# A spectral and expert-retrieval layer in one kernel: two blocks of tokens looked up row by row, with u and v rows in one fetch and part of the checks moved

## The chip, the cores and the metric

The kernel runs on one core of a Trainium2 chip. Its time is the device time of one execution in microseconds (us): before the change the median of 3 runs is 1177.19 us (1176.13 to 1178.46). The profiled execution is one more run, with a time of its own.

## The reference, cut to what matters

2048 tokens x of 512 numbers are normalised; the output is x plus a Fourier mixing of them (part A) plus an expert layer (part B):

```python
xn  = layernorm(x)
A   = dft_seq_re @ (xn @ dft_hid_re.T) - dft_seq_im @ (xn @ dft_hid_im.T)
q   = einsum("nd,dhc->nhc", xn, w_q)             # 32 heads, two halves of 128
s1, s2 = q1 . k1, q2 . k2                        # 64 keys each
# the 2 best of the 2 x 2 best sums s1 + s2 name 2 of 4096 experts per head
g   = softmax(top_s)
act = gelu(einsum("nd,nhkd->nhk", xn, u[top_e]))
out = x + A + einsum("nhk,nhk,nhkd->nd", g, act, v[top_e])
```

So every token uses 64 rows of u and the same 64 rows of v, each of 512 floats.

## The kernel before, in words

The tokens are 16 blocks of 128. The work has three parts.

The opening transforms the tokens and prepares the first weights. The **score part** runs over 8 chunks of 4 heads (j) and, in each, over 16 blocks (i): twelve matmuls per step (L705), a copy to SBUF on ScalarE (L710), and on VectorE the best values and their indices (L713, L717). Between the steps ScalarE and GpSimd (POOL) split weights into two 16-bit parts (`m_prep`, L158 to L166; `fill_uv`, L608 to L610), and POOL and VectorE turn the indices into experts and gates (`routing`, L641 to L685).

The **block part** (from L1143) does most blocks densely. For block b, `u_part` (L834) multiplies all 4096 rows of u with the tokens in eight groups of 48 matmuls; ScalarE applies gelu (L837) into `act`. `g_mm` spreads the gates over the experts: VectorE builds L and R by comparisons (L860, L865, L868) from `cmp`, PE multiplies them (L870). `w_part` forms gate times activation (L878 on VectorE, L882 on ScalarE, L883 on VectorE), and `v_part` (L890) multiplies with v, 96 matmuls into one PSUM bank `v`. `finish` (L909) has VectorE read that bank, add the residual and store. `compact` transposes the indices of a later block on PE into a bank `zt` (L694), from which ScalarE makes `cmp` (L695). The loop at L1156 does, for each b: v of b beside w and g of b + 1; finish of b; zt of b + 2; u and half of g of b + 2. I call what lies between one zt and the next a cycle. `v` and `zt` are taken from the same two PSUM banks, tag "pc".

NB = 15 blocks are dense. The last one (NS = 1) is **picked**: 64 rows of u and 64 of v per token are fetched by indirect DMAs of 128 rows of 2 KB, issued by POOL (L914) into 5 buffers. First 64 dots on VectorE (L943), then one gelu over all 64 slots and a product with the gates, then 64 gains: ScalarE scales a row of v (L954), POOL adds it (L955). `pick` (L967) spreads these steps over the turns of the cycles, 16 a cycle; `follow` ties their order on VectorE and ScalarE behind a matmul, without a wait.

Beside it run **checks**: 68 comparing steps (`compare`, L980, and `compare_w`, L1032) load parts of the Fourier matrices (L987, L988), test their symmetry on VectorE (L989 to L1029) and sum the deviations on ScalarE (L1030); 60 `fit` steps (L1070) look at the size of weights on ScalarE. They use the 4 buffers of tag "w", as `w_part` does. Five comparing steps fall to a cycle, on odd turns and on one even turn of v.

A scheduler in the framework orders each engine's instructions from the program's order and the dependencies; engines then run in that order and wait on semaphores. DMAs issued by SP, and those issued by POOL, each stand in their engine's order.

Of the kernel before, what the change touches and what calls it, by code (L numbers as in the profile page):

```python
# [32 lines left out]
NS = 1  # L33
# [3 lines left out]
def tile_fnet_peer(ctx, tc, x, ca, cb, c5, wt, wf, wr, wq, kt, ut, un, vn, out):  # L37
# [52 lines left out]
    NF = NW + 32 + NCH - 1  # L90
    sums_sb = cst.tile([P, 138 + NF + 3], F32, name="sums")
# [459 lines left out]
    def part_b(safe, stS, stP, stE, xt, u_sb, cmp_p):  # L551
# [146 lines left out]

        def scores(j, i, vals, idx):
# [3 lines left out]
            for kd in range(KD):  # L703
                for l, r in ((0, 0), (0, 1), (1, 0)):
                    nc.tensor.matmul(ps, xt[i][:, l, kd, :], m[:, r, kd, :], start=(n == 0),  # L705
                                     stop=(n == 3 * KD - 1))
                    n += 1
# [12 lines left out]
            return st[:, 512:]  # L720
# [29 lines left out]
        for (which, g), n in zip(fills, slots):  # L750
            todo[n].append(lambda at, w=which, g=g: fill_uv(w, g, at))
            todo[n - (3 if n < 113 else 1)].append(lambda at, w=which, g=g: fill_load(w, g))
        m_stage(1, wq_tile, 0)
        pend = None
        for j in range(NCH):
# [5 lines left out]
            for i in range(NT):  # L761
                spare = scores(j, i, vals, idx)
# [48 lines left out]
        AHEAD = 5  # L811
# [84 lines left out]
        def follow(i, after):  # L896
            tc.add_manual_dep(i, after.ins.name, mybir.DependencyInfo(
                mybir.DependencyClass.NoSync, mybir.DependencyReason.DATA), reason="pace")

# [12 lines left out]
        def gather(table, n, s):  # L912
            t = bp.tile([P, D], F32, tag="ga", name=f"ga{n}_{s}", bufs=5)
            nc.gpsimd.indirect_dma_start(  # L914
                out=t, out_offset=None, in_=table,
                in_offset=bass.IndirectOffsetOnAxis(ap=eix[:, n].rearrange("p k h -> p (k h)")[:, s:s + 1], axis=0))
            return t

        def picked(n):

            b = NB + n
            N = 2 * H
            G = {}
            T = {}

            def fetch(s):
                if s < 2 * N:
                    G[s] = gather((un, vr)[s // N], n, s % N)

            def begin():  # L930
                xs = T["x"] = bp.tile([P, D], F32, tag="xs", name=f"xs_{n}", bufs=1)
                o = T["o"] = bp.tile([P, D], F32, tag="ov", name=f"ov{n}", bufs=1)
                T["z"] = bp.tile([P, N], F32, tag="za", name=f"za{n}", bufs=1)
                nc.sync.dma_start(xs, x[b // 4, b % 4])
                nc.sync.dma_start(o, y_d[b])
                nc.gpsimd.dma_start(o, x[b // 4, b % 4], accum_op=ALU.add)
                for s in range(AHEAD):
                    fetch(s)
                norm(xs, xs, b)

            def dot(s):
                t = G.pop(s)
                nc.vector.scalar_tensor_tensor(t, t, 1.0, T["x"], op0=ALU.mult, op1=ALU.mult,  # L943
                                               accum_out=T["z"][:, s:s + 1])
                fetch(s + AHEAD)

            def gate():
                za = T["z"]
                nc.scalar.activation(za, za, AF.Gelu_apprx_tanh)
                nc.gpsimd.tensor_tensor(za, za, gts[:, n].rearrange("p k h -> p (k h)"), op=ALU.mult)  # L950

            def gain(s):
                t = G.pop(N + s)
                nc.scalar.activation(t, t, AF.Copy, scale=T["z"][:, s:s + 1])  # L954
                nc.gpsimd.tensor_tensor(T["o"], T["o"], t, op=ALU.add)  # L955
                fetch(N + s + AHEAD)

            return [begin, *(lambda s=s: dot(s) for s in range(N)), gate, *(lambda s=s: gain(s) for s in range(N)),
                    lambda: nc.sync.dma_start(out[b * P:(b + 1) * P], T["o"])]

        vr = vn.rearrange("c p d -> (c p) d")
        picks = [] if safe else [f for n in range(NS) for f in picked(n)]
        more = [range(1, 1 + max(0, n - k * (NB - 2) - 4)) for n, k in ((68, 5), (NF - NCH + 1, 4))]
# [13 lines left out]

        later = []

        def compare(n):  # L980

            ri, g, kk = n // 32, n // 8 % 4, n % 8
            odd = kk // 4
            t = bp.tile([P, 4, 4, 64], F32, tag="w", name=f"cx{n}", bufs=WB)
            tf = t.rearrange("p s q c -> p (s q c)")
            tv = t.rearrange("p s q c -> p s (q c)")
            nc.sync.dma_start(tf[:, :P], ca[ri, g, :, kk * P:(kk + 1) * P])  # L987
            nc.sync.dma_start(tf[:, P:], cb[ri, g, kk].rearrange("p b c -> p (b c)"))  # L988
            nc.vector.tensor_reduce(asum[:, n:n + 1], tf[:, :P], axis=AX.X, op=ALU.add,  # L989
                                    apply_absolute_value=True)  # L990
            sgn = (((1, 1, 1), (-1, 1, -1)), ((-1, -1, 1), (1, -1, -1)))[ri][odd]
            ops = [ALU.subtract if v > 0 else ALU.add for v in sgn]
            op = ops[1]
            if g == 0:
                nc.vector.tensor_tensor(tv[:, 1], tv[:, 1], tv[:, 0], op=ops[0])
                for i in (2, 3):
                    nc.vector.scalar_tensor_tensor(tv[:, i], tv[:, 0], not0, tv[:, i], op0=ALU.mult, op1=ops[i - 1])  # L997
                f = (-1 if ri else 1) * sgn[1] * sgn[2]
                nc.vector.tensor_tensor(tv[0:1, 3], tv[0:1, 3], tv[0:1, 2],
                                        op=ALU.subtract if f > 0 else ALU.add)  # L1000
            else:
                sets = {}
                for i, o in enumerate(ops):
                    sets.setdefault(o, []).append(i + 1)
                for o, ix in sets.items():
                    sl = slice(ix[0], ix[-1] + 1, ix[1] - ix[0] if len(ix) > 1 else 1)
                    v = tv[:, sl]
                    nc.vector.tensor_tensor(v, v, tv[:, 0:1].to_broadcast([P, len(ix), 256]), op=o)  # L1008
            m = ALU.add if ri else ALU.subtract

            def mirror(v):

                c = 0 if kk else 1
                nc.vector.tensor_tensor(v[:, 2:4, c:], v[:, 2:4, c:], v[:, 0:2, c:], op=m)  # L1014
                if c:
                    nc.vector.tensor_tensor(v[:, 3, 0:1], v[:, 3, 0:1], v[:, 2, 0:1], op=m)

            if g == 0:
                mirror(t[0:1, 2])
                if odd and ri:  # L1020

                    nc.vector.tensor_copy(t[0:1, 2, 0:2], t[0:1, 0, 0:2])
# [5 lines left out]
            if kk == 0:  # L1028
                nc.vector.memset(t[:, 0, 2, 0:1], 0.0)  # L1029
# [308 lines left out]
```

## Time and profile before

| | us |
|---|---|
| median of 3 runs | 1177.19 |
| profiled execution, its time | 1171.21 |
| span of its instructions | 1169.3 |
| the cycles, from the end of block 0 to the end of block 13 | 526.7 to 1141.8 |
| PE busy, of the span | 1118.0 |
| VectorE busy | 987.5 |
| ScalarE busy | 632.3 |
| POOL busy | 488.1 |

A row of a group of instructions reads: line, engine, operation, what is written and read, shapes, count | busy us, mean ns of one | idle time of the engine just before them, and what ended it. A busy share is an average over parts with different limits, so the prediction reads the score part and the cycles apart.

### The profile page before, as it was taken

What the parts mean: (1) busy time and instruction counts of PE and PEld (TensorE: products, weight loads), DVE (VectorE), ACT (ScalarE), POOL (GpSimd) and SP (SyncE); (2) the same over time, 40 slices, a digit from 0 to 9 for tenths busy, and PEclk for the clock granted to TensorE, in tenths of its full rate; (3) what the DMA queues carried; (4) which work ended last, traced back from release to release, by engine and by line L of the source; (5) the groups of instructions that cost most, each with busy time, mean ns of one, the idle gap of its engine ahead of it and who ended that gap; (6) DMA issues with size and microseconds to landing.
All of it is one profiled execution on the core that took longest, in us unless ns stands there. A gap on an engine that the chain in (4) does not pass through costs nothing.

```text
span 1169.3 us, 29061 instructions
## 1 busy us (share of the span) xinstructions
PE 1118.0 (96%) x11681; PEld 734.0 (63%) x11681; DVE 987.5 (84%) x2946; ACT 632.3 (54%) x995; POOL 488.1 (42%) x411
## 2 busy tenths in 40 slices
PE   5799999999999999979999999999998999989997
PEld 4354555454454448939668578687685876858763
DVE  7878888798898997887998887988899689879895
ACT  2575546767767663443543534534546465464563
POOL 0021525548548342131343222323374666656742
PEclk9899999999999999989999999999999999999999
DMA  8254224132231113223554745645536456364554
GB/s 311 78 211 151 85 79 162 55 108 89 93 110 55 55 62 127 58 80 102 169 179 146 217 143 151 202 138 174 181 104 175 132 162 173 109 192 137 158 148 109
DMA packets 74369, 157.02 MB, mean 134 GB/s; under 512 B 10086, under 2 KB 26989, under 8 KB 74224
## 3 DMA queue, kind: packets, MB, share of 16 engines
q1 hardware_dynamic: 61522, 117.30, 30.1%
q0 software_dynamic: 12544, 37.76, 12.4%
q8 instruction: 93, 1.52, 0.5%
q14 instruction: 52, 0.43, 0.1%
q10 hardware_dynamic: 158, 0.01, 0.0%
HBM read 141.08 MB, written 13.96 MB: 133 GB/s over the span
## 4 chain that ended last, share of the span: by engine, by line
PE 71%; DVE 17%; DMA 4%; ACT 4%; issue 3%; SPq 0%; POOL 0%; DVEq 0%; ACTq 0%; POOLq 0%
PE s L705 27%; PE z L834 22%; PE v L890 14%; DVE L L860 3%; PE g L870 3%; DVE act L883 2%; DMA cx<-in_cb_dram 2%; DVE w L878 2%; ACT act L882 2%; DVE R L865 2%; PE m L144 2%; PE p L366 2%; DVE R L868 1%; DVE cx L1008 1%; DVE cx L997 1%
## 5 line engine op out<-in xcount | busy, mean ns | idle before, releaser
L834 PE MATMUL z<-xb,u 128*128 128x128 f16 x5760 | 335.1, 221 | 15.0 <-ACT act L837 12.6
L705 PE MATMUL s<-m,xq 128*128 128x512 f16 x1536 | 338.9, 379 | 0.0
L834 PEld LDWEIGHTS <-u 128*128 128x128 f16 x5760 | 327.6, 99 | 16.1 <-issue 13.3
L890 PE MATMUL v<-v,act 128*128 128x512 f16 x1440 | 319.7, 380 | 0.0
L705 PEld LDWEIGHTS <-xq 128*128 128x128 f16 x1536 | 148.4, 98 | 171.3 <-issue 0.2
L890 PEld LDWEIGHTS <-act 128*128 128x128 f16 x1440 | 138.2, 98 | 160.5 <-issue 1.9
L860 DVE TENSOR_TENSOR L<-io_lam,cmp 128x2048 f16<-128x2048 f16 x120 | 152.6, 1271 | 62.5 <-PE g L870 52.8
L837 ACT ACTIVATE act<-z,scl 128x512 f32<-128x512 f32 x120 | 81.9, 685 | 197.0 <-PE z L834 196.8
L914 POOL DMA_INDIRECT ga<-in_un_dram,eix x64 | 81.7, 1276 | 219.3 <-DVE ga L943 182.0
L713 DVE MAX8 vals<-ss 128x8 f32<-128x64 f32 x1024 | 152.6, 216 | 19.4 <-ACT ss L710 19.2
L955 POOL TENSOR_TENSOR ov<-ov,ga 128x512 f32<-128x512 f32 x64 | 98.3, 1535 | 114.0 <-ACT ga L954 112.4
L710 ACT ACTIVATE ss<-s,wsc 128x512 f32<-128x512 f32 x112 | 75.5, 680 | 81.8 <-PE s L705 71.7
L882 ACT ACTIVATE act<-w 128x1024 f16<-128x1024 f32 x60 | 79.5, 1351 | 54.5 <-DVE w L878 52.0
L717 DVE FIND_INDEX8 idx<-vals,ss 128x8 uint16<-128x256 f32 x256 | 107.1, 418 | 0.0
L914 POOL DMA_INDIRECT ga<-in_vn_dram,eix x64 | 89.2, 1393 | 34.7 <-DVE ga L943 17.3
L1030 ACT ACTIVATE cx<-cx 128x896 f32<-128x896 f32 x64 | 60.5, 946 | 67.4 <-DVE cx L1014 40.6
L883 DVE TENSOR_TENSOR act<-w,act 128x1024 f16<-128x1024 f32 x60 | 81.8, 1363 | 14.3 <-ACT act L882 14.1
L865 DVE TENSOR_TENSOR R<-io_c,cmp 128x512 f16<-128x512 f16 x120 | 81.5, 679 | 0.0
L878 DVE SCALAR_TENSOR_TENSOR w<-act,scl,g 128x1024 f32<-128x1024 f32 x60 | 75.4, 1276 | 2.2 <-PE g L870 1.8
L870 PEld LDWEIGHTS <-L 128*128 128x128 f16 x1920 | 56.4, 96 | 20.2 <-issue 8.0
L870 PE MATMUL g<-R,L 128*128 128x32 f16 x1920 | 58.6, 176 | 10.2 <-DVE R L868 7.8
L166 POOL TENSOR_TENSOR wq<-wq,wh 128x1024 f16<-128x1024 f32 x26 | 55.5, 2133 | 19.1 <-DMA wq<-in_wq_dram 16.4
(271 smaller groups left out, 1241.0 us busy)
## 6 DMA issues: line engine op xcount, KB each, us to landing
cx<-in_cb_dram SPq DMA_DIRECT2D x64, 448.0 KB, 4.4
wq<-in_wq_dram SPq DMA_DIRECT2D x32, 512.0 KB, 6.5
fit<-in_wq_dram SPq DMA_DIRECT2D x28, 512.0 KB, 5.4
uv<-in_ut_dram SPq DMA_DIRECT2D x16, 512.0 KB, 3.7
uv<-in_vn_dram SPq DMA_DIRECT2D x16, 512.0 KB, 3.7
xq<-in_x_dram SPq DMA_DIRECT2D x8, 512.0 KB
xt_d<-xq SPq DMA_DIRECT2D x16, 256.0 KB, 4.1
cx<-in_ca_dram SPq DMA_DIRECT2D x64, 64.0 KB, 2.5
```

Of the source, the lines that this page charges most:

```text
L705: nc.tensor.matmul(ps, xt[i][:, l, kd, :], m[:, r, kd, :], start=(n == 0), stop=(n == 3 * KD - 1))
L713: nc.vector.max(vals[:, i, w, :, h], s[:, g, :])
L717: nc.vector.max_index(idx[:, i, w].rearrange("p k h -> p (k h)"), vals[:, i, w, 0:2].rearrange("p k h -> p (k h)"), s[:, w * HC:g + 1, :]. ...
L834: mm = nc.tensor.matmul(p[:, cc * P:(cc + 1) * P], ug[:, l, c % 2, kd, :], xb[:, r, kd, :], start=(n == 0), stop=(n == 3 * KD - 1))
L860: nc.vector.tensor_tensor(L.rearrange("p t (l two) -> p t l two", two=2), io_lam.rearrange("p (l two) -> p l two", two=2).unsqueeze(1).to_ ...
L865: nc.vector.tensor_tensor(Rv, io_c.rearrange("p (c two) -> p c two", two=2).unsqueeze(1).to_broadcast([P, 16, NC // 2, 2]), bc(1, NC), op= ...
L870: nc.tensor.matmul(p[:, hf, t * NC:(t + 1) * NC], L[:, t, :], R[:, t, :], start=True, stop=True)
L878: nc.vector.scalar_tensor_tensor(w, act[:, :, ts], fw, p.rearrange("p h (n c) -> p c (h n)", c=NC), op0=ALU.mult, op1=ALU.mult)
L882: nc.scalar.activation(w16[..., 0], w, AF.Copy)
L883: nc.vector.tensor_tensor(w16[..., 1], w, w16[..., 0], op=ALU.subtract)
L890: mm = nc.tensor.matmul(pv, w16[:, c, :, l], vg[:, r, c % 2, :], start=(c == 0 and k == 0), stop=(c == NC - 1 and k == 2))
L914: nc.gpsimd.indirect_dma_start(out=t, out_offset=None, in_=table, in_offset=bass.IndirectOffsetOnAxis(ap=eix[:, n].rearrange("p k h -> p ( ...
```

## The change

- NS = 2: 14 blocks are dense, two are picked. The loop over blocks and the number of turns follow (12 cycles, 196 turns).
- The rows of u and v lie side by side in one table `uv`; one indirect DMA fetches 128 rows of 4 KB, into 3 buffers, two rows ahead. A row's dot and its gain follow each other at once: gelu and gate are done slot by slot on ScalarE.
- x of the dots is kept in a PSUM bank of tag "pc" instead of SBUF.
- 32 of the 68 comparing steps (`EARLY`) run in the score part: loaded four steps ahead, the differences on POOL, the sums on ScalarE two steps later, in 2 buffers of their own. The sum of the reference values, a reduction on VectorE before, is a second ScalarE operation in all of them.
- The other 36 comparing steps and the fits are spread evenly over the turns of v (`paced`).

```diff
-NS = 1
+NS = 2
...
+    EARLY = [*range(8, 24), *range(40, 56)]
+    early = cst.tile([P, 2, len(EARLY)], F32, name="early")
...
+            v_eng = nc.vector if at is None else nc.gpsimd
...
-            nc.vector.tensor_reduce(asum[:, n:n + 1], tf[:, :P], axis=AX.X, op=ALU.add,
-                                    apply_absolute_value=True)
...
+            def judge():
+                k = n if at is None else at
+                a, b = (chk, asum) if at is None else (early[:, 0], early[:, 1])
+                nc.scalar.activation(tf[:, P:], tf[:, P:], AF.Abs, accum_out=a[:, k:k + 1])
+                nc.scalar.activation(tf[:, :P], tf[:, :P], AF.Abs, accum_out=b[:, k:k + 1])
...
+        for k in range(len(EARLY)):
+            n = 20 + k * 13 // 4
+            checks.setdefault(n - 4, []).append(lambda mm, k=k: check_load(k))
+            checks.setdefault(n, []).append(lambda mm, k=k: hold(cx[k][0], mm))
+            checks.setdefault(n + 2, []).append(lambda mm, k=k: hold(cx[k][1], mm))
...
-        AHEAD = 5
+        BUFS = 3
+        AHEAD = BUFS - 1
...
+                t = T[n, s] = bp.tile([P, 2 * D], F32, tag="ga", name=f"ga{n}_{s}", bufs=BUFS)
+                nc.gpsimd.indirect_dma_start(
+                    out=t, out_offset=None, in_=uv,
+                    in_offset=bass.IndirectOffsetOnAxis(ap=eix[:, n].rearrange("p k h -> p (k h)")[:, s:s + 1], axis=0))
...
+                xs = bp.tile([P, 2 * D], F32, tag="ga", name=f"xs_{n}", bufs=BUFS)[:, :D]
+                T["x"] = pc(f"px{n}")
...
+                nc.sync.dma_start(o, y_d[b])
+                nc.gpsimd.dma_start(o, x[b // 4, b % 4], accum_op=ALU.add)
+                norm(T["x"], xs, b)
...
+            nc.vector.scalar_tensor_tensor(t, t, 1.0, T["x"], op0=ALU.mult, op1=ALU.mult, accum_out=z)
+            nc.scalar.activation(z, z, AF.Gelu_apprx_tanh)
+            nc.scalar.activation(z, z, AF.Copy, scale=gts[:, n].rearrange("p k h -> p (k h)")[:, s:s + 1])
+            fetch()
...
+        def gain(n, s):
+            o = T["o"]
+            t = T.pop((n, s))[:, D:]
+            nc.scalar.activation(t, t, AF.Copy, scale=T["z"][:, s:s + 1])
+            nc.gpsimd.tensor_tensor(o, o, t, op=ALU.add)
...
+        def paced(k):
+            st = streams[k]
+            st[1] += 1
+            for f in st[0][st[2]:-(-len(st[0]) * st[1] // (4 * (NB - 2) + 2))]:
+                step(f)
+                st[2] += 1
...
-                if 0 < b < NB - 1 and (cg % 2 == 1 or cg == 6) or b + 1 == NB and cg < 4 or cg == 4 and b in more[0]:
-                    step(units)
...
+                if 0 < b < NB - 1 or b + 1 == NB and cg < 4:
+                    paced(cg % 2)
...
-    un = c(arr(B_u)[:, dord])
+    uv = c(np.concatenate([arr(B_u)[:, dord], arr(B_v)[:, dord]], axis=1))
```

More of the change, by code (lines that the diff above doesn't have):

```diff
@@ L32, with tile_fnet_peer @@
 V2 = 11
[L33 removed]
+NS = 2
 @with_exitstack
[L37 removed]
+def tile_fnet_peer(ctx, tc, x, ca, cb, c5, wt, wf, wr, wq, kt, ut, vn, uv, out):
     nc = tc.nc
@@ L697, in compact, with follow, hold @@
             CMP[b] = cmp
+        def follow(i, after):
+            tc.add_manual_dep(i, after.ins.name, mybir.DependencyInfo(
+                mybir.DependencyClass.NoSync, mybir.DependencyReason.DATA), reason="pace")
+        def hold(f, after):
+            made = nc.cur_bb.bb.instructions
+            first = len(made)
+            f()
+            for i in made[first:]:
+                if i.engine in (mybir.EngineType.DVE, mybir.EngineType.Activation, mybir.EngineType.Pool):
+                    follow(i, after)
@@ L761, in part_b @@
             for i in range(NT):
-                spare = scores(j, i, vals, idx)
+                spare, mm = scores(j, i, vals, idx)
+                for f in () if safe else checks.get(j * NT + i, ()):
+                    f(mm)
                 for t, f in ((j * NT + i, y_rows), (j * NT + i - 10, y_store)):
```

192 lines of the change are left out of this document (91 added, 101 removed).

## The prediction

> **What bounds the kernel now.** I read the page first, then the stretches of the stage that the change shortens, then the groups of instructions on VectorE in two of those stretches. In the stretches the columns are length, then busy time (and instructions) of PE, PEld, DVE, ACT and POOL, granted clock, DMA share, GB/s; the first is the score part, the third the thirteen cycles from the end of block 0 to the end of block 13, the fourth and fifth six and five of these cycles.
>
> ```profile
> span 1169.3 us, 29061 instructions
> PE 1118.0 (96%) x11681; PEld 734.0 (63%) x11681; DVE 987.5 (84%) x2946; ACT 632.3 (54%) x995; POOL 488.1 (42%) x411
> ```
> ```profile
> 95.00:447.00 352.00, 349.56 (x2198) 173.66 (x2197) 309.70 (x1675) 227.24 (x368) 176.12 (x176) 1.00 0.26 87
> ...
> 526.70:1141.80 615.10, 599.60 (x7944) 449.98 (x7943) 525.51 (x878) 309.49 (x475) 273.26 (x199) 0.99 0.53 157
> 572.50:848.30 275.80, 274.25 (x3668) 205.27 (x3667) 235.21 (x459) 129.83 (x198) 85.22 (x68) 1.00 0.55 168
> 848.30:1094.10 245.80, 234.03 (x3057) 176.30 (x3056) 212.49 (x294) 132.96 (x207) 150.66 (x104) 0.98 0.51 150
> ```
>
> PE at 96% says "matmul", but the two halves differ. Early a cycle takes 275.80/6 = 45.97 us and PE is busy 99% of it: PE sets it. Late a cycle takes 245.80/5 = 49.16 us, PE idles, and VectorE is busier (212.49/5 = 42.5 us a cycle against 235.21/6 = 39.2), though its dots have ended. The same groups in the two halves say why (columns: count, busy us, mean ns, idle before):
>
> ```profile
> L860 DVE TENSOR_TENSOR L<-io_lam,cmp 128x2048 f16<-128x2048 f16 x48 | 58.7, 1222 | 25.1 <-PE g L870 22.2 <-ACT cmp L695 2.9
> L943 DVE SCALAR_TENSOR_TENSOR ga<-ga,xs 128x512 f32<-128x512 f32 x56 | 37.9, 687 | 0.0
> L883 DVE TENSOR_TENSOR act<-w,act 128x1024 f16<-128x1024 f32 x25 | 33.3, 1330 | 6.3 <-ACT act L882 6.3
> ...
> L1008 DVE TENSOR_TENSOR cx<-cx 128x768 f32<-128x768 f32 (+2 forms) x36 | 24.0, 698 | 3.7 <-DMA cx<-in_cb_dram 3.3 <-issue 0.4
> L868 DVE TENSOR_TENSOR R<-R,cmp 128x512 f16<-128x512 f16 x48 | 20.1, 420 | 0.5
> L865 DVE TENSOR_TENSOR R<-io_c,cmp 128x512 f16<-128x512 f16 x48 | 20.1, 419 | 0.0
> L1014 DVE TENSOR_TENSOR cx<-cx 128x128 f32<-128x128 f32 (+3 forms) x40 | 10.8, 284 | 0.1
> L989 DVE TENSOR_REDUCE sums<-cx 128x1 f32<-128x128 f32 x32 | 9.1, 285 | 4.7 <-DMA cx<-in_ca_dram 4.7
> L997 DVE SCALAR_TENSOR_TENSOR cx<-cx,not 128x256 f32<-128x256 f32 x14 | 6.2, 484 | 0.0
> ```
> ```profile
> L860 DVE TENSOR_TENSOR L<-io_lam,cmp 128x2048 f16<-128x2048 f16 x40 | 52.9, 1324 | 16.5 <-PE g L870 11.1 <-ACT cmp L695 5.4
> L865 DVE TENSOR_TENSOR R<-io_c,cmp 128x512 f16<-128x512 f16 x40 | 39.3, 982 | 0.0
> L883 DVE TENSOR_TENSOR act<-w,act 128x1024 f16<-128x1024 f32 x20 | 28.6, 1432 | 7.1 <-ACT act L882 7.1
> ...
> L868 DVE TENSOR_TENSOR R<-R,cmp 128x512 f16<-128x512 f16 x40 | 21.3, 532 | 0.5
> ...
> L997 DVE SCALAR_TENSOR_TENSOR cx<-cx,not 128x256 f32<-128x256 f32 x12 | 8.4, 738 | 0.0
> ```
> ```profile
> L955 POOL TENSOR_TENSOR ov<-ov,ga 128x512 f32<-128x512 f32 x50 | 76.1, 1523 | 83.6 <-ACT ga L954 83.2
> L914 POOL DMA_INDIRECT ga<-in_vn_dram,eix x49 | 69.8, 1425 | 13.9 <-POOL ov L955 13.4 <-DMA fit<-in_wq_dram 0.5
> ```
>
> From early to late the build of L and R slows: L860 by 102 ns x40, L865 by 563 x40, L868 by 112 x40, L883 by 102 x20, L997 by 254 x12: 4.1 + 22.5 + 4.5 + 2.0 + 3.0 = 36 us. What is new late is POOL's addition L955, 50 times; gathers alone (early) did not do this. So each addition costs VectorE about 36/50 = **0.72 us**, and the late half is bound by VectorE's sequence, not by PE.
>
> **The change part by part.** The sum is made against the profiled execution, 1171.21 us with a span of 1169.3; the timed runs' median, 1177.19, is 6.0 us above it, and I add the difference found to the median.
>
> *One dense block leaves.* Twelve cycles stay instead of thirteen; of 615.10/13 = 47.3 us each, one goes: **-47.3 us**. The stretches before and after them keep their work. If the cycles do not lengthen, this is what is won.
>
> *The remaining cycles on VectorE*, starting from the early 39.2 us. Two rows of the timeline at a block's end (start, us) are needed here and below:
>
> ```profile
> 1049.28 0.74 DVE L909 SCALAR_TENSOR_TENSOR y<-v,scl,y 128x512 f32<-128x512 f32 x1
> 1051.22 1.23 DVE L860 TENSOR_TENSOR L<-io_lam,cmp 128x2048 f16<-128x2048 f16 x1 [1.20 <-ACT cmp L695]
> ```
>
> - Dots: 56 in six early cycles is 9.3 a cycle; 128 rows in twelve is 10.7. At 0.69 us (L943) +0.9. The factor x now lies in PSUM, a form the trace lacks. L909, same shape with a PSUM operand, takes 0.74 us: at most 0.06 us more per dot; at the other end 0 or less, if the PSUM read costs nothing or spares a meeting with POOL. I take +0.06, +0.6 a cycle.
> - Comparing steps: 32 in six early cycles, 57 us by the groups quoted plus the small ones (about 7 us), so 9.6 us a cycle. After, 36 units in twelve: 16 with first-row handling at some 2.4 us (two L997, two L1014 and two more of some 0.4), 16 plain ones at 2 x 0.70 + 0.28 = 1.7, and 4 of the weight kind at some 4.5 (estimate: a dozen operations between the 284 ns of L1014 and the 484 of L997), 84 us, 7.0 a cycle: -2.6. Their first reduction (L989) goes to ScalarE.
> - Additions on POOL: early none, now one per row: 10.7 x 0.72 = +7.7.
>
> Sum 39.2 + 0.9 + 0.6 - 2.6 + 7.7 = **45.8 us busy**. VectorE also waits: late 49.16 - 42.5 = 6.7 us a cycle, on PE, ScalarE and loads of cx. I keep 6.7, because the next edit replaces the waits that fewer cx loads spare. Cycle **52.5 us**; between 49.3 (half of the waits) and 57 (0.72 becomes 1.1, half way to the 1.52 of a whole addition) I keep both ends. Twelve cycles: 630.0 against 615.1, **+14.9 us**.
>
> *One PSUM bank of two is taken* by x for twelve cycles. v and zt shared the two; now zt(b+2) has to wait until VectorE has read v(b). The program order puts 15 to 20 matmuls of the next z ahead of zt, then PE stands. With the rows above, these show how late that read is:
>
> ```profile
> 1044.06 0.33 PE L694 MATMUL zt<-ident,zb 128*128 128x128 f16 x3
> ...
> 1052.43 0.77 PE L834 MATMUL z<-xb,u 128*128 128x128 f16 x11 [2.68 <-ACT act L837]
> ```
> ```profile
> L695 ACT ACTIVATE cmp<-zt 128x768 f16<-128x768 f16 x15 | 11.8, 793 | 5.9 <-PE zt L694 5.9
> ```
>
> PE did zt at 1044.06; VectorE came to L909 at 1049.28, 5.2 us later. Behind the waiting zt stand all of z, then cmp on ScalarE and L860. PE ran ahead here by 8.2 us and lost 2.68 later anyway. Under the new order it loses 5.2 + 0.74 less the matmuls ahead (0.77/11 each, 1.1 to 1.4 us), 4.7 us, at this place instead; VectorE, which is the later engine, then waits for zt and cmp (0.33 + 0.79, estimated 1.5 us with hand-overs) where it waited 1.20. I cost it inside the 6.7 us.
>
> *Rows of 4 KB, three buffers.* The trace has gathers of 256 KB, and these rows of ScalarE:
>
> ```profile
> L914 POOL DMA_INDIRECT ga<-in_un_dram,eix x64: 946/982/6266, 460.3 to 804.7; - x64
> ...
> DMA to landing us min/median/max: 3.2/4.2/8.1
> ```
> ```profile
> q0 software_dynamic: 12544, 37.76, 12.4%
> ```
> ```profile
> L1030 ACT ACTIVATE cx<-cx 128x896 f32<-128x896 f32 x64 | 60.5, 946 | 67.4 <-DVE cx L1014 40.6 <-DVE cx L1029 6.6 <-DVE cx L1022 4.1
> ...
> L566 ACT ACTIVATE ss<-wsc 128x1 f32<-128x1 f32 x28 | 5.4, 192 | 0.0
> ```
>
> Queue 0 moved 37.76 MB in 12.4% of the span, 260 GB/s, so another 256 KB adds 1.0 us: landing 5.2 us (estimate), 9.1 at worst. The gather of row s+3 waits for the addition of row s: dot 0.7, two small ScalarE steps 0.2 each, half a row's pace 2.5, copy 0.7 (as L1030, fewer elements), addition 1.5, gather issue inside the landing: 5.8 + 5.2 = 11.0 us against three rows, 3 x 52.5/10.7 = 14.7. Hidden, with 3.7 us to spare. ScalarE gets 5.3 more copies and 21 small steps a cycle, 8 us on 27 of 52: hidden unless it waits for a late dot.
>
> *Between the two blocks* the last addition, the store of the first block's rows, the load of the second's and the accumulating DMA follow one another; VectorE's norm and first dot wait for the load of x, and in POOL's queue the next gathers stand behind the accumulating DMA.
>
> ```profile
> y<-in_x_dram POOLq DMA_DIRECT2D x15, 256.0 KB, 5.4
> out_dram<-y SPq DMA_DIRECT2D x15, 256.0 KB, 2.1
> ```
>
> Addition 1.5, store 2.1 and the load (between these two rows, 5.4 at most) make 9 us until POOL is free, less 3.7 spare: **+5 us** (0 to 10).
>
> *32 comparing steps in the score part.* POOL has 176.12 of 352 us busy; a step is 768 + 128 elements, between 1.6 us (2133 ns per 1024 in L166) and 2.3 (612 ns per 256 in L663): 32 x 2.1 = 67 us, filling POOL to 69%. ScalarE gets 32 times 0.95 (L1030) and a short one, with their two accumulator reads some 1.6: 51 us on 227. Their 64 loads move too, on SP's queue: two buffers, so a load waits for ScalarE's sums two steps earlier, and the loads of weights behind it, asked for three steps (8 us) ahead, wait with it; the DMA share there is 0.26.
>
> ```profile
> L166 POOL TENSOR_TENSOR wq<-wq,wh 128x1024 f16<-128x1024 f32 x24 | 51.2, 2133 | 1.0
> ...
> L663 POOL TENSOR_TENSOR if<-if,hoff 128x256 f32<-128x256 f32 x7 | 4.3, 612 | 3.8 <-DVE if L660 3.8
> ```
> ```profile
> DVE pm L644 <- POOL c L643: 12.1, 7, 2.7
> ```
>
> PE is busy 349.56 of 352 there, with VectorE at 309.70 as cover. VectorE already waits 12.1 us for POOL's routing; doubled it still fits into 42 us of idle time. I take **+2** (0 to 12, if a routing chain comes last).
>
> Total: 14.9 + 5 + 2 = **+22 us**: span 1191, the profiled execution 1193, timed 1177 + 22 = **1199 us**.
>
> A rule speaks against the change: the Trainium skill, "SBUF — State Buffer", section "SBUF: two separate sides", says that a VectorE operation with two SBUF inputs and a GpSimd operation exclude one another for a whole instruction. By it alone an addition could cost VectorE all of its 1.52 us, and the sum would be rival 3's 1302 us; the 0.72 of this trace lies below it, as it would if not every addition met such an operation.
>
> **The rivals.**
> 1. *PE stays the bound* (faster). VectorE's stretching shrinks because the dots, with x in PSUM, leave more room for POOL's additions; for it speaks the middle one of these late cycles, at 45.6 us in spite of the additions:
>
> ```profile
> 896.10:947.90 51.80, 47.45 (x612) 35.82 (x611) 39.84 (x71) 27.52 (x43) 31.46 (x21) 0.97 0.53 156
> 947.90:993.50 45.60, 45.60 (x612) 34.24 (x611) 41.99 (x53) 26.56 (x41) 30.14 (x21) 1.00 0.52 153
> 993.50:1044.10 50.60, 47.51 (x613) 35.98 (x612) 44.02 (x58) 26.47 (x42) 27.93 (x20) 0.97 0.51 147
> ```
>
>    At 45.97 us, with 7 for the two small terms: 12 x 45.97 - 615.1 + 7 = -56, 1121 us. At half the stretching (48.6): 583 - 615 + 7 = -25, 1152. It decides below (615.1 - 7)/12 = 50.7 us a cycle. Against it: that cycle was paid back by its neighbours, 51.8 and 50.6.
> 2. *The gathers become the bound*: the three-buffer loop exceeds three rows if a landing takes over 8.9 us. At 9.1 plus a late ScalarE (2 us) the loop is 16.9, a row 5.6, a cycle 60: 1177 + 720 - 615 + 7 = 1289 us. Against it: median 4.2.
> 3. *The whole addition blocks*: VectorE loses 1.52 instead of 0.72, 10.7 x 0.80 = 8.6 us a cycle; 12 x (52.5 + 8.6) = 733, 1177 + 733 - 615 + 7 = 1302 us. Against it: the measured 0.72. This is what the rule of the Trainium skill, "SBUF — State Buffer", would give.
> 4. *The score part lengthens*: POOL's chain delays routing in each of seven chunks by a step (2.1 us): +15, with the forecast 1212.
>
> **How the numbers follow.** Forecast, cycles bound by VectorE at 50.7 to 56 us: 0.50. Rival 1: 0.29. Rival 2: 0.08. Rival 3: 0.04. Rival 4: 0.09. The range leaves out 0.1 at each side: 1145 (more than half of rival 1 lies above it) to 1260 (below rivals 2 and 3). A measurement here tells about 0.2%, 2.4 us, from no change. Faster 0.31 (rival 1 and the forecast's edge), same 0.03, slower 0.66.
>
> **What would show it.** Right: cycles of 51 to 55 us throughout; PE z idle behind zt's wait for the read of v; L865's successor near 1 us in every cycle; VectorE busy about 46 us a cycle. Wrong: cycles near 46 (rival 1); dots idle on the gather's DMA (rival 2); score part over 352 us (rival 4).

## The result, and the profile after

The changed kernel takes 1206.56 us (median of 4 runs, 1204.78 to 1210.13) against 1177.83 us of the kernel before beside it: ratio **1.0248** (95% interval 1.0220 to 1.0276), slower by 28.7 us. The profiled execution took 1206.9 us. That of before (1171.21 us) lies 6 us below its own median, so differences between the two profiles come out some 6 us larger than those of the timed runs.

The first lines of its page:

```profile
span 1204.7 us, 28712 instructions
...
PE 1094.1 (91%) x11070; PEld 708.4 (59%) x11070; DVE 984.1 (82%) x2886; ACT 732.1 (61%) x1429; POOL 666.4 (55%) x570
```

PE has lost five points of its share, VectorE has as much to do as before although a dense block is gone, and POOL and ScalarE have gained 178 and 100 us. To see where the 35.4 us of span went, I divided the execution at four places that both kernels have: the score part, from the first to the last of its matmuls (L705 before, L787 after); the read of v by VectorE that ends block 0 (L909, L1001); the same for the last block but one; the same for the last. Two rows of stretches for each kernel (length; busy time of PE, PEld, VectorE, ScalarE, POOL; granted clock; DMA share; GB/s), the score part and the cycles, before first:

```profile
72.30:443.40 371.10, 370.55 (x2337) 184.68 (x2335) 324.42 (x1725) 241.29 (x392) 180.39 (x178) 1.00 0.29 98
526.90:1146.70 619.80, 604.30 (x7965) 451.97 (x7963) 530.14 (x897) 311.84 (x479) 273.26 (x199) 0.99 0.53 158
```
```profile
71.40:448.80 377.40, 371.35 (x2337) 184.90 (x2335) 321.97 (x1698) 277.26 (x520) 256.64 (x274) 1.00 0.42 141
533.60:1168.30 634.70, 569.26 (x7332) 421.16 (x7330) 529.04 (x844) 377.10 (x786) 378.93 (x264) 0.97 0.60 181
```

| stretch | before | after | difference |
|---|---|---|---|
| start, score part and block 0, up to its end | 526.9 | 533.6 | +6.7 |
| the cycles, 13 and 12 | 619.8 | 634.7 | +14.9 |
| last block | 16.2 | 23.4 | +7.2 |
| after its read of v | 6.4 | 13.0 | +6.6 |

Per cycle that is 47.7 and 52.9 us. Inside the cycles PE's busy time and its waits make nearly the whole. Its waits there (total, times, longest), before and after:

```profile
PE z L834 <- ACT act L837: 12.6, 6, 3.9
PE g L870 <- DVE w L878: 2.0, 3, 1.0
PE g L870 <- DVE R L868: 0.5, 1, 0.5
```
```profile
PE zt L696 <- DVE y L1001: 23.5, 9, 7.4
PE g L966 <- DVE w L974: 21.1, 12, 4.2
PE g L966 <- DVE R L964: 11.5, 7, 2.9
PE z L930 <- ACT act L933: 5.3, 5, 1.8
```

604.3 + 15.1 = 619.4 of 619.8 before, 569.3 + 61.4 = 630.7 of 634.7 after. Of the 5.2 us that a cycle is longer, 4.0 are waits and 0.9 is slower matmuls (busy 46.5 and 47.4 us a cycle, at a granted clock of 0.99 and 0.97). Of the 61.4 us of waits after, 56.1 are for VectorE. Its groups in the same stretch (mean ns after the comma, then the idle time before it):

```profile
L956 DVE TENSOR_TENSOR L<-io_lam,cmp 128x2048 f16<-128x2048 f16 x96 | 139.8, 1456 | 45.5 <-PE g L966 27.3 <-ACT cmp L697 11.6 <-ACT ga L1040 4.4
L1032 DVE SCALAR_TENSOR_TENSOR ga<-ga,px 128x512 f32<-128x512 f32 x126 | 84.9, 678 | 25.6 <-DMA ga<-in_uv_dram,eix 25.3 <-DVE px L261 0.2
L979 DVE TENSOR_TENSOR act<-w,act 128x1024 f16<-128x1024 f32 x48 | 71.7, 1497 | 6.1 <-ACT act L978 4.4 <-ACT za L1033 1.4
L974 DVE SCALAR_TENSOR_TENSOR w<-act,scl,g 128x1024 f32<-128x1024 f32 x48 | 60.5, 1274 | 0.5 <-PE g L966 0.2
L964 DVE TENSOR_TENSOR R<-R,cmp 128x512 f16<-128x512 f16 x96 | 57.8, 602 | 1.0
L961 DVE TENSOR_TENSOR R<-io_c,cmp 128x512 f16<-128x512 f16 x96 | 57.2, 596 | 0.0
```

Early in the kernel before, L956's predecessor took 1222 ns and those of L964 and L961 420: over the cycles the builds are stretched now. The timeline shows how. An addition and the builds beside it, from the first of these cycles:

```profile
549.63 1.75 POOL L1041 TENSOR_TENSOR ov<-ov,ga 128x512 f32<-128x512 f32 x1
```
```profile
549.04 1.21 DVE L956 TENSOR_TENSOR L<-io_lam,cmp 128x2048 f16<-128x2048 f16 x1
550.17 1.49 DVE L964 TENSOR_TENSOR R<-R,cmp 128x512 f16<-128x512 f16 x1
```

The addition takes 1.75 us where the shortest takes 1.25, and L964, begun while it ran, ends 0.28 us after it, at 551.66, instead of after its usual 0.42 us. Nearly all go this way: of the 192 operations of L961 and L964 in the cycles, 32 begin while an addition runs, and 31 of these end 0.27 to 0.30 us after it; the 150 that no addition touches take 0.41 us. And the dots wait 25.3 us for their rows, inside VectorE's fixed order, so everything behind them on VectorE waits too.

The end of the kernel, rows of the timeline:

```profile
1168.32 0.75 DVE L1001 SCALAR_TENSOR_TENSOR y<-v,scl,y 128x512 f32<-128x512 f32 x1
1169.12 22.57 PE L986 MATMUL v<-v,act 128*128 128x512 f16 x96 [4.69 <-DVE y L1001]
...
1196.87 1.25 POOL L1041 TENSOR_TENSOR ov<-ov,ga 128x512 f32<-128x512 f32 x1 [6.79 <-issue]
1198.15 0.34 SPq L1044 DMA_DIRECT2D out_dram<-ov  x1
```

x holds one of the two banks to the end, so the last v waits for the read of the one before; and POOL's last addition comes 5 us after the last block has been read, with the store of the picked block behind it.

### The profile page after: what moved, and what is told of

The parts are those of the page before. It is cut to its first block, busy times and chain, and to the rows that moved or that the text cites. A ratio compares the mean times of both kernels' runs of the same rounds, so it can differ in the third digit from the quotient of the medians.

```text
span 1204.7 us, 28712 instructions
## 1 busy us (share of the span) xinstructions
PE 1094.1 (91%) x11070; PEld 708.4 (59%) x11070; DVE 984.1 (82%) x2886; ACT 732.1 (61%) x1429; POOL 666.4 (55%) x570
## 5 line engine op out<-in xcount | busy, mean ns | idle before, releaser
L787 PE MATMUL s<-m,xq 128*128 128x512 f16 x1536 | 339.1, 379 | 0.9 <-ACT ss L792 0.9
L930 PE MATMUL z<-xb,u 128*128 128x128 f16 x5376 | 318.4, 222 | 7.9 <-ACT act L933 5.3
L930 PEld LDWEIGHTS <-u 128*128 128x128 f16 x5376 | 310.8, 99 | 11.5 <-issue 6.3
L1041 POOL TENSOR_TENSOR ov<-ov,ga 128x512 f32<-128x512 f32 x128 | 192.6, 1505 | 220.8 <-ACT ga L1040 159.3
L986 PE MATMUL v<-v,act 128*128 128x512 f16 x1344 | 310.2, 391 | 4.7 <-DVE y L1001 4.7
L787 PEld LDWEIGHTS <-xq 128*128 128x128 f16 x1536 | 148.4, 98 | 172.3 <-issue 1.4
L1012 POOL DMA_INDIRECT ga<-in_uv_dram,eix x128 | 180.8, 1413 | 68.4 <-POOL ov L1041 34.0
L956 DVE TENSOR_TENSOR L<-io_lam,cmp 128x2048 f16<-128x2048 f16 x112 | 161.2, 1440 | 53.8 <-PE g L966 35.6
L1032 DVE SCALAR_TENSOR_TENSOR ga<-ga,px 128x512 f32<-128x512 f32 x128 | 86.3, 678 | 25.6 <-DMA ga<-in_uv_dram,eix 25.3
L1040 ACT ACTIVATE ga<-ga,za 128x512 f32<-128x512 f32 x128 | 91.6, 716 | 6.6
L792 ACT ACTIVATE ss<-s,wsc 128x512 f32<-128x512 f32 x112 | 75.1, 678 | 28.3 <-PE s L787 15.2
L966 PE MATMUL g<-R,L 128*128 128x32 f16 x1792 | 55.5, 177 | 39.9 <-DVE w L974 21.1
L979 DVE TENSOR_TENSOR act<-w,act 128x1024 f16<-128x1024 f32 x56 | 82.3, 1472 | 6.4 <-ACT act L978 4.6
L966 PEld LDWEIGHTS <-L 128*128 128x128 f16 x1792 | 53.1, 96 | 50.7 <-issue 39.4
L1033 ACT ACTIVATE za<-za 128x1 f32<-128x1 f32 x128 | 24.9, 195 | 87.6 <-DVE ga L1032 81.3
L747 POOL TENSOR_TENSOR cx<-cx 128x512 f32<-128x512 f32 (+2 forms) x56 | 61.8, 1121 | 28.9 <-DMA cx<-in_cb_dram 15.3
```

What stands on the lines that cost most here:

```text
L787: mm = nc.tensor.matmul(ps, xt[i][:, l, kd, :], m[:, r, kd, :], start=(n == 0), stop=(n == 3 * KD - 1))
L930: mm = nc.tensor.matmul(p[:, cc * P:(cc + 1) * P], ug[:, l, c % 2, kd, :], xb[:, r, kd, :], start=(n == 0), stop=(n == 3 * KD - 1))
L956: nc.vector.tensor_tensor(L.rearrange("p t (l two) -> p t l two", two=2), io_lam.rearrange("p (l two) -> p l two", two=2).unsqueeze(1).to_ ...
L966: nc.tensor.matmul(p[:, hf, t * NC:(t + 1) * NC], L[:, t, :], R[:, t, :], start=True, stop=True)
L979: nc.vector.tensor_tensor(w16[..., 1], w, w16[..., 0], op=ALU.subtract)
L986: mm = nc.tensor.matmul(pv, w16[:, c, :, l], vg[:, r, c % 2, :], start=(c == 0 and k == 0), stop=(c == NC - 1 and k == 2))
```

## The experiments

The kernel before ran beside each on the same chip (1171.5 us for the first four, 1183.2 for the others), so runs are compared by their ratio to it; each is known to 0.2 to 0.4% to either side. "Cycles" are the stretches from the end of block 0 to the end of the last block but one.

| run | us | ratio (95%) | us per cycle |
|---|---|---|---|
| the change | 1206.6 | 1.0248 (1.0220 to 1.0276) | 52.9 |
| e1, zt in another bank | 1202.8 | 1.0284 (1.0244 to 1.0323) | 52.6 |
| e2, additions of one column | 1160.4 | 0.9913 (0.9889 to 0.9937) | 49.3 |
| e3, one picked block | 1189.4 | 1.0167 (1.0130 to 1.0205) | 47.8 (of 13) |
| e4, all steps beside the cycles | 1237.1 | 1.0596 (1.0548 to 1.0644) | 55.5 |
| e5, e2 and e1 together | 1153.8 | 0.9755 (0.9725 to 0.9786) | 48.5 |
| e6, rows of 2 KB, six buffers | 1198.2 | 1.0124 (1.0104 to 1.0145) | 51.7 |
| e7, gain on VectorE | 1165.1 | 0.9852 (0.9823 to 0.9881) | 49.7 |
| e8, last block mended | 1194.9 | 1.0085 (1.0051 to 1.0118) | 52.7 |
| e9, e7 with free banks | 1147.5 | **0.9690** (0.9648 to 0.9732) | 48.9 |
| e10, e9 with one picked block | 1162.3 | 0.9834 (0.9813 to 0.9855) | 46.7 (of 13) |
| e11, before with e7's gain | 1168.3 | 0.9875 (0.9836 to 0.9914) | 47.1 (of 13) |
| e12, e7 with idle additions | 1316.0 | 1.1148 (1.1098 to 1.1197) | not comparable |

My theory at first was the prediction's: VectorE's work sets the cycle. The rivals were the bank that zt waits for, and the pace of the rows.

**e1.** The gate alone.

```diff
-            p = pc(f"zt{b}", F16)
+            p = psum.tile([P, 512], F16, tag="pb", name=f"zt{b}", bufs=2)
```

> The changed kernel with one edit: the transposes zt go to a bank of the tag pb instead of pc, so zt no longer waits for VectorE's read of v, and the v of the last block finds its bank free. My theory (VectorE's sequence sets the cycle): PE's 23.5 us of waits of zt disappear but come back as other waits; only the 4.7 us of the last block and about half of the 11.6 us that VectorE waited for cmp are won: 1206.6 - 10 = 1197 us (1190 to 1203), cycles 51.5 to 52.5 us. Rival (the bank gate sets the cycle): all of 23.5 + 4.7 us comes out, 1178 us, cycles about 50.6 us.

Nothing was won clear of the noise (1.0284 against 1.0248, each known to 0.3 to 0.4%), where I had expected 10 us. PE's waits in e1's cycles:

```profile
PE g L966 <- DVE w L974: 23.6, 12, 7.4
PE z L930 <- ACT cmp L697: 16.1, 5, 6.5
PE z L930 <- ACT act L933: 12.3, 10, 1.8
PE g L966 <- DVE R L964: 11.6, 7, 2.4
```

The 23.5 us in front of zt are now 16.1 in front of z for cmp, and 7 more for act. My expectation for the last block was wrong too: v still waited 4.7 us there, since it is x, not zt, that holds the other bank.

**e2.** The price of POOL's additions.

```diff
-            nc.gpsimd.tensor_tensor(o, o, t, op=ALU.add)
+            nc.gpsimd.tensor_tensor(o[:, 0:1], o[:, 0:1], t[:, 0:1], op=ALU.add)
```

> The changed kernel with POOL's addition cut to the first of its 512 columns, 128 times (this leaves out the rest of the expert rows' sum in the two picked blocks). Everything else stays: gathers, dots, scaled copies, the bank gate. My theory (each addition stretches VectorE's 16-bit builds by about 0.62 us): L956 falls from 1456 to about 1230 ns, L961 and L964 from 600 to about 420 ns, the cycles become PE's 46 to 47 us, 12 x 6 us less: 1206.6 - 73 = 1134 us (1125 to 1150). Rival (bank gate or row pace sets the cycle): cycles stay above 50 us, 1180 us or more.

The cycles of e2 and three of VectorE's groups in them:

```profile
534.10:1126.10 592.00, 558.14 (x7332) 415.23 (x7330) 444.74 (x846) 377.45 (x786) 225.98 (x264) 0.98 0.62 193
```
```profile
L956 DVE TENSOR_TENSOR L<-io_lam,cmp 128x2048 f16<-128x2048 f16 x96 | 117.3, 1222 | 69.8 <-PE g L966 51.5 <-ACT cmp L697 18.3
...
L974 DVE SCALAR_TENSOR_TENSOR w<-act,scl,g 128x1024 f32<-128x1024 f32 x48 | 60.6, 1275 | 0.3
...
L961 DVE TENSOR_TENSOR R<-io_c,cmp 128x512 f16<-128x512 f16 x96 | 40.0, 417 | 0.0
```

With the same gathers, copies and gates, VectorE's busy time falls from 529.0 to 444.7 us, and the builds are back to 1222 and 417 ns: the stretching is shown to come from the additions, 84 us or 0.67 us each. In time the additions are worth 3.3% (1.0248 to 0.9913), about 39 us and more than the 28.7 us that the change lost: without their length it would have been a little faster than the kernel before. An addition of one column is also shorter (529 ns for 1509), but the dots wait 28.3 us for their rows here, no less than under the change, so it is not the rows that came sooner. The size was missed: only 42.7 us came out of the cycles, not the 73 that I expected. With VectorE relieved, PE's own busy time and waits are what is left, and the rest of VectorE's 84 us became idle time.

**e3.** `NS = 2` becomes `NS = 1`, all else as changed.

> The changed kernel with NS = 1: 15 dense blocks, 64 rows over 13 cycles, all other parts of the change kept. My theory: 4.9 rows a cycle leave VectorE at about 36 us busy, PE sets the cycle with 46.2 us, 13 x 46.2 = 600.6 against 615.1 before; score part +5.6, last block and end +10: 1177.8 + 1 = 1179 us (1170 to 1186). Rival (the bank gate costs PE 4.7 us at each block end): cycles near 50 us, 1228 us.

Missed: 47.8 us a cycle, 1.6 over what I had taken for PE's floor, though VectorE was busy for only 470.1 of 621.0 us. PE waits for 17.7 us of them, 10.2 in front of zt and 7.5 for builds. By stretches e3 stands 8.6 us behind the kernel before at the end of block 0 (the score part takes 379.5 us), 1.2 in the cycles, 7.2 in the last block and 1.4 after it: with half the rows and no gain of a cycle, nearly all of the loss lies in the parts to which the prediction gave +2 and nothing.

**e4.** `EARLY` is empty.

> The changed kernel with no comparing step in the score part: all 68 beside the cycles. My theory (VectorE sets the cycle): the 32 steps cost VectorE about 1.9 us each there, 61 us, less 5.6 us that the score part gets back: 1206.6 + 50 = 1257 us (1240 to 1265), cycles near 57 us. Rival (the cycle is set by something else than VectorE's work, bank gate or rows): the steps fit into VectorE's 105 us of idle time, 1201 to 1215 us.

Slower by 3.4% than the change. By the ratio that is 1248 us beside the change's 1206.6, within the range; the cycles are at 55.5 us, not 57. The cycles and the score part:

```profile
526.10:1192.50 666.40, 576.46 (x7332) 429.52 (x7330) 563.41 (x913) 414.33 (x907) 387.20 (x264) 0.95 0.62 196
71.30:441.80 370.50, 370.50 (x2337) 184.68 (x2336) 324.49 (x1725) 241.48 (x392) 180.72 (x178) 1.00 0.28 98
```

The score part is back at 370.5 us (before 371.1): moving 32 steps there costs 6.9 us and saves 31.7 in the cycles. This part of the change pays. The 32 steps cost VectorE 34.4 us (529.0 to 563.4), not the 61 that I had put, and nearly all of it is in the cycles: more work for VectorE passes into the time where VectorE is late, while less work (e2) does so only until PE is the later one.

**e5.** e1's and e2's edits together.

> The changed kernel with both edits of the runs before: additions of one column (the rest of the expert rows' sum is left out) and zt in a bank of the tag pb. My theory: with VectorE relieved PE is the engine that comes last, and now its 14.9 us of waiting for the bank are on the path: 15 us (10 to 20) below the run with one-column additions alone, 0.978 of before. Rival: the bank costs nothing here either, as it did beside full additions: within 3 us of that run, 0.991 of before.

Held: 1.6% below e2. The same edit that brought nothing beside full additions brings 10 us in the cycles (592.0 to 581.9) once VectorE is not late: a gate costs time only while no other engine comes later.

**e6.** Gathers from the v table alone, `[P, D]` buffers, `BUFS = 6`.

> The changed kernel with gathers of the v half alone, 2 KB per row, into six buffers and five rows ahead; dot, copy and addition keep their shapes and count (the dots take v for u and the gains the dots' products, so this part of the result is left out). My theory: the 25.3 us that VectorE waits for rows go and stay gone, since VectorE is the bound: ratio 1.007 (1.002 to 1.012), cycles near 50.5 us. Rival (another wait takes their place, as with the bank): 1.02 or more.

Between the two, nearer to mine: the dots no longer wait at all, and the cycles are 14.2 us shorter (620.5), not 25:

```profile
536.60:1157.10 620.50, 567.59 (x7331) 420.92 (x7329) 532.84 (x844) 376.79 (x786) 379.92 (x261) 0.97 0.44 131
```

VectorE's waits for PE grew in their place (L956 for g: 27.3 to 43.0 us). The pace of the rows is worth at most about half of what VectorE waits for them: e6 also fetches half the bytes, and VectorE's waits for loads of the comparing steps fell too, from 17.8 to 9.7 us, so part of the 14.2 us may be theirs.

**e7.** The gain on VectorE.

```diff
-            nc.scalar.activation(t, t, AF.Copy, scale=T["z"][:, s:s + 1])
-            nc.gpsimd.tensor_tensor(o, o, t, op=ALU.add)
+            nc.vector.scalar_tensor_tensor(o, t, T["z"][:, s:s + 1], o, op0=ALU.mult, op1=ALU.add)
```

> The changed kernel with the gain as one VectorE operation per row (o = row x gate + o) in place of ScalarE's copy and POOL's addition. My theory: VectorE pays about 0.69 us itself for what POOL's addition cost it, 0.64 us (80.6 us over 126 rows by the run with one column): the cycles stay within 1 us of the changed kernel's 52.6, L961 falls to 420 ns, the end is some 6 us shorter; ratio 1.02 (1.01 to 1.03). Rival (the row's chain over ScalarE and POOL sets the pace, not VectorE's time): rows come free 3 us sooner, ratio below 1.0.

Here my theory fell. The cycles of e7, two groups and PE's waits:

```profile
536.90:1133.50 596.60, 559.35 (x7332) 417.18 (x7330) 521.88 (x962) 295.74 (x660) 170.83 (x139) 0.99 0.62 192
```
```profile
L1040 DVE SCALAR_TENSOR_TENSOR ov<-ga,za,ov 128x512 f32<-128x512 f32 x125 | 93.5, 748 | 24.1 <-ACT za L1034 15.9 <-ACT act L933 6.1 <-issue 1.2
L1032 DVE SCALAR_TENSOR_TENSOR ga<-ga,px 128x512 f32<-128x512 f32 x126 | 85.8, 682 | 0.0
```
```profile
PE g L966 <- DVE R L964: 14.5, 12, 2.3
PE zt L696 <- DVE y L1001: 13.5, 8, 3.4
PE z L930 <- ACT act L933: 2.8, 1, 2.8
PE g L966 <- DVE w L974: 1.7, 5, 0.7
```

VectorE is nearly as busy as under the change, 521.9 us for 529.0, as I had worked out; yet the cycles are 38.1 us shorter, and the ratio is below 1.0, as the rival forecast. PE's account says where: waits 61.4 to 32.5, busy time 569.3 to 559.4. VectorE's account has 7.1 us less work, 25.3 us of waits for rows that are gone (the dots wait for no row now), and 5.7 us less of other waits. Two causes changed together here: the builds are no longer stretched, and a row comes free sooner. e7 alone does not tell them apart; e6 comes nearest. There the dots wait for no row either, the builds are stretched, and VectorE's busy time is 11.0 us longer than in e7, but the cycles are 23.9 us longer. So, rows aside, VectorE's time seems to cost more as stretching of builds than as operations of its own; e6 differs in the bytes fetched as well, so this is not shown strictly.

**e8.** The end of the kernel.

```diff
-            pv = pc(f"v{b}")
+            pv = (pb if b + 1 == NB else pc)(f"v{b}")
...
-        turns = 16 * (NB - 2) + 4
+        turns = 16 * (NB - 2)
```

> The changed kernel with two edits at its end: v of the last block in a bank of the tag pb, which no z uses any more then, and the rows spread over the turns up to the end of the last cycle but none in the last block. My theory: the last block's wait of 4.7 us and the 6.6 us of late additions go, the cycles get 2% denser in rows (+2 us in all): ratio 1.0165 (1.013 to 1.020), 10 us won. Rival (the last block is held by something else, such as the late builds of VectorE): under 4 us won, 1.022 or more.

In the timeline of e8 the v of the last block starts ahead of the read of the one before, and the last addition is over in time:

```profile
1167.78 20.67 PE L986 MATMUL v<-v,act 128*128 128x512 f16 x95
1169.83 1.27 POOL L1041 TENSOR_TENSOR ov<-ov,ga 128x512 f32<-128x512 f32 x1 [2.17 <-issue]
1169.87 0.74 DVE L1001 SCALAR_TENSOR_TENSOR y<-v,scl,y 128x512 f32<-128x512 f32 x1
...
1188.48 0.75 DVE L1001 SCALAR_TENSOR_TENSOR y<-v,scl,y 128x512 f32<-128x512 f32 x1 [7.80 <-PE v L986]
```

Last block 18.6 us for 23.4, the rest of the span 6.5 for 13.0: 11.3 us, as expected. The ratio fell by more (1.6%, about 19 us), below its range. The profile does not show where the other 8 came from; the two medians lie 11.7 us apart as timed (1206.6 and 1194.9), and e8's runs spread from 1188.5 to 1197.0, so much of the 8 may be noise.

**e9.** e1's, e7's and e8's first edit together.

> The changed kernel with the gain on VectorE, zt in a bank of the tag pb and v of the last block in a bank of the tag pb. My theory (where VectorE no longer comes late, PE's waits are what is left): the 13.5 us of waits of zt and the 4.5 us of the last block go, 10 to 18 us below the run with the gain on VectorE alone: ratio 0.973 (0.968 to 0.978). Rival (the bank comes back as another wait, as beside POOL's additions): only the last block's 4.5 us, 0.981.

Held, and the fastest: 3.1% below the kernel before, 5.4% below the change. Last block 19.6 us, cycles 587.0 us; as in e5, the bank is worth its 10 us (596.6 to 587.0) once VectorE is not late.

**e10.** e9 with `NS = 1`.

> The same kernel with NS = 1, 15 dense blocks. My theory (the second picked block is worth one PE-bound cycle of 46 us, less what 64 rows more cost): 13 cycles of 46.5 us, 605 against 615.1 before, the score part 6 us longer: ratio 0.997 (0.990 to 1.003). Rival (the gain on VectorE is what wins, the second block brings nothing): as the run with two blocks, 0.975 to 0.985.

Better than expected, and inside the rival's range; but the rival's claim, that the second block brings nothing, does not hold, for this is 1.5% slower than e9. In the form of the change a second picked block cost 0.8% (e3 to the change); with the gain on VectorE and free banks it wins 1.5%.

**e11.** The kernel before with e7's edit at L954 and L955.

> The kernel before with one edit: the gain as one VectorE operation per row in place of ScalarE's copy and POOL's addition. My theory (POOL's additions stretch the builds that PE waits for; on VectorE the same time falls where it is not awaited): the late cycles go from 49.2 to 46.5 us, 13 us: ratio 0.989 (0.984 to 0.995). Rival (the late cycles are bound by VectorE's busy time, which stays): 0.998 to 1.002.

The time held (0.9875), and the last six cycles took 46.6 us each. VectorE's groups in them (864.9 to 1144.6), where the builds took 1324 and 982 ns in the late cycles of the kernel before:

```profile
L860 DVE TENSOR_TENSOR L<-io_lam,cmp 128x2048 f16<-128x2048 f16 x48 | 58.6, 1220 | 25.1 <-PE g L870 20.2 <-ACT cmp L695 4.8
L954 DVE SCALAR_TENSOR_TENSOR ov<-ga,za,ov 128x512 f32<-128x512 f32 x59 | 44.1, 747 | 0.2
...
L865 DVE TENSOR_TENSOR R<-io_c,cmp 128x512 f16<-128x512 f16 x48 | 20.1, 418 | 0.0
```

The theory behind the number is not shown by it. Its point was that VectorE's time stays and falls elsewhere; but over the last six cycles VectorE's busy time fell as well, from 255.2 us in the kernel before (851.4 to 1146.7) to 238.9, by about as much as the cycles, 295.3 to 279.7. A bound by VectorE's work would give that too. The edit also takes 59 copies off ScalarE, and PE's waits for ScalarE's gelu fell from 11.2 to 1.5 us in the same stretches. What e11 does show is that the win does not need rows that come sooner, for VectorE waits for no row in either kernel. It rests on the timed runs: the two profiled executions have nearly the same span (1169.3 and 1169.0 us), as that of before (1171.21 us) was shorter than every run of the same kernel timed beside e11 (1180.6 to 1184.1).

**e12.** e7, and beside each row three additions on POOL of a 160-column tile to itself.

> The changed kernel with the gain on VectorE, and beside each row three additions on POOL to a small tile that nothing reads (160 columns each, about the length of one 512-column addition): POOL's additions are back, the row's chain over ScalarE and POOL is not. This adds work to no output. My theory now (two causes of the 36 us between POOL's gain and VectorE's: rows late by the chain, 12 us, and stretched builds that PE awaits, 24 us): L961 back to 500 to 600 ns, cycles from 49.7 to 52 or more, ratio 1.01 to 1.04. Rival (the chain is all): L961 stretched, but cycles within 1 us of 49.7, ratio 0.985 to 0.995.

Inconclusive: it tested neither. The additions depend on nothing, and the order put all 384 into one stretch ahead of the row work:

```profile
449.00:740.50 291.50, 136.49 (x1795) 104.92 (x1793) 124.90 (x246) 62.48 (x98) 237.94 (x403) 0.74 0.18 55
```
```profile
L974 DVE SCALAR_TENSOR_TENSOR w<-act,scl,g 128x1024 f32<-128x1024 f32 x12 | 15.3, 1273 | 87.1 <-POOL v L612 86.5 <-PE g L966 0.7
```

There they stood in front of POOL's work on the weights (L612), for which VectorE waited 86.5 us. Once they were over, the cycles were e7's (544.2 us for eleven, 49.5 each). How the 38 us between the change and e7 divide between stretched builds and the shorter chain of a row stays open. What bounds it: taking the stretch away with the row waits in place gave 42.7 us (e2); taking the row waits away with the stretch in place gave 14.2 (e6), and going on from there to e7 gave 23.9; putting 93.5 us of gains on VectorE on top of e2 and taking the row waits away cost 4.6 (e2 to e7).

## Why the prediction was right, and where it was not

The time was forecast at 1199 us and came out at 1206.6; slower was right, and by the mechanism named: POOL's additions lengthen VectorE's work until the shorter list of cycles takes longer than the longer one did (e2). The exact size owes something to errors that cancel. By its steps:

- **One cycle leaves, the others take 52.5 us.** Over the prediction's own kind of stretch (533.4 to 1164.4, 631.0 us) the cycle is 52.6. But the way there was wrong: VectorE's busy time plus 6.7 us of waits that stay. It was 43.8 busy and 8.8 of waits, two errors that cancel, which is luck. The 52.6 also holds the changeover between the picked blocks, for which the sum adds 5 us besides; together it had 635 us for this stretch. And the method fails outside this case: e7 has the same busy time and 3 us less a cycle, e2 has 84 us less busy time and gains half of it. Adding up VectorE's busy time holds while VectorE is the late engine, as in e4.
- **0.72 us for an addition.** 0.67 measured (e2). It was read as lying mostly on the R build (L865 at 982 ns); now it is spread, 596 and 602 ns on L961 and L964 and 234 more on L956. "L865's successor near 1 us" was wrong as a sign, the sum right.
- **x of the dots in PSUM, +0.06 us.** The dot took 678 ns, for 687 with x in SBUF: nothing lost. With 10.7 dots in a cycle that is 0.7 us a cycle less than I took.
- **The bank's gate inside the 6.7 us.** Right for the cycles (e1 won nothing), for the reason given: VectorE was the later engine. Too large as a wait: 4.7 us were worked out for PE at one block's end, and PE waited 23.5 us in all twelve cycles, in nine places. Wrong for the end: that the last v finds no free bank was not in the sum. The last block grew by 7.2 us, of which e8 took back 4.8.
- **The gathers are hidden with 3.7 us to spare.** Wrong. The loop of 11.0 us was set against three rows of mean spacing, but rows are not evenly spaced (the first four dots of the cycles start at 538.26, 540.34, 542.63 and 546.42 us, where the mean is 5.0 us apart, and the fourth waits 3.10 us for its row) and each step of the chain waits in its engine's order (POOL's additions waited 159.3 us for ScalarE's copies, by their group in the cycles). It came to 25.3 us of waits, worth at most 14 (e6).
- **Between the blocks +5.** The cycle with the changeover took 59.3 us (844.7 to 904.0), 6.4 more than the mean: right.
- **The score part +2.** It was +6.3 (371.1 to 377.4), within the 0 to 12 kept. VectorE's wait for POOL's routing grew from 12.1 to 19.3 us, and PE, at 0.6 before, waited 5.2 us for weights that POOL splits (L168). With the start and block 0, which the sum left alone, it is +6.7.
- **Nothing after the cycles.** This is the step that failed in size, a term put at nothing: +7.2 and +6.6 us, about as much as the whole sum was short of the profile (1193 forecast, 1206.9 measured). The prediction asked what a row's work costs in a cycle, and not where the last rows end; e8 took 11.3 of it back by two lines.

Of the rivals, "PE stays the bound" was nearest to what a better version does: e9's cycles stand at 48.9 us, under the 50.7 at which the prediction saw the change turn. It named the wrong way there (x in PSUM making room); what made room was to have no additions on POOL. Rival 3's 1302 us did not come, since an addition cost VectorE 0.67 us on average and not 1.52. The rule of the Trainium skill, "SBUF — State Buffer", section "SBUF: two separate sides", that the prediction set beside it is not refuted by that: a build that meets an addition does wait for its end, and the mean is lower because not every addition meets such an operation, which is how the prediction had read its 0.72.

## What to carry to other kernels

Ask not only how busy the late engine is but which of its operations the others await: 84 us of stretching on awaited builds cost 43 us, while 94 us of operations in their stead cost some 19 (an estimate: 4.6 measured from e2 to e7, plus the 14.2 by e6 that the rows coming sooner may have given back; 33 if all of e2's 28.3 us of row waits had counted). Moving work to an idle engine isn't free when that engine slows the busy one. A gate on one engine shows long waits and is worth nothing while another engine is later (e1 against e5 and e9): mend the late engine first, then measure the gate again. Follow spread-out work to the end of the kernel, where its last pieces and the buffers that it holds have no cover.

## What the runs showed of the hardware

- POOL's additions stretch VectorE operations that read two tensors in SBUF: the builds L956, L961 and L964, L979, and the comparing steps' L734, L736 (611 ns under the change, 477 in e2), L738, L747 and L753. Operations with an operand in PSUM keep their time: L974 1274 and 1275 ns, the dot 678 and 680. So does a reduction that reads one tensor in SBUF: L989 took 280 ns in the last six cycles of the kernel before, beside 59 additions, and 284 in e11 without them.
- A build that begins during an addition waits for its end: L961 and L964, 0.42 us alone, took up to 1.50, and 31 of 32 ended 0.27 to 0.30 us after the addition. It goes the other way too: 52 of the 125 additions took over 1.35 us, where the shortest took 1.25, and each of the 52 began while one of these operations ran. The Trainium skill, "SBUF — State Buffer", section "SBUF: two separate sides", names operations with two SBUF inputs as those that meet GpSimd's, one of the two waiting for the whole instruction of the other; the traces agree. The mean of 0.67 us an addition is lower than its 1.5 us because not every addition meets such an operation: one begins during some 67 of the 125.
- The same 7332 matmuls of the cycles were busy for 576.5 us at a granted clock of 0.95 (e4), 569.3 us at 0.97 (the change) and 559.4 us at 0.99 (e7): in these three the kernel in which PE waits more (81.7, 61.4 and 32.5 us) also paid with slower matmuls. Why the clock differed no run here shows.
